# A retention layer and a gated MLP on one core: who loads, scales and turns each visit, and in which order

## The chip, the cores and the metric

The kernel runs on one core of one Trainium2 chip. The core has five engines with a queue of instructions each: TensorE (PE, matrix products and transposes), VectorE (DVE), ScalarE (ACT), GpSimd (POOL) and SyncE (SP, which here only issues transfers). Each queue runs in its order; an instruction that waits holds up everything behind it. ACT and POOL can issue transfers as well. The metric is the device time of one execution in microseconds, lower is better. Every time below is of this kernel before the change, either its timed runs or one profiled execution.

## The reference

For 8 batches, 8 heads, 576 positions and head size 64, the first half is a retention layer, scores masked by a decay and multiplied with the values, with no softmax. The second half is a gated MLP over the sequence; all inputs and the output are float32.

```python
scores = (1.0 / np.sqrt(D)) * np.matmul(q, k.transpose(0, 1, 3, 2))
gamma = 1.0 - 2.0 ** (-5.0 - np.arange(H))
Dmat = np.where(rel >= 0, gamma[:, None, None] ** rel, 0.0)      # rel = i - j
x = merge_heads(np.matmul(scores * Dmat, v))                      # 8 x 576 x 512
h = gelu_tanh(x @ w_in)                                           # 8 x 576 x 1024
u, v = h[..., :512], h[..., 512:]
v_n = (v - mean(v)) / np.sqrt(var(v) + 1e-6) * g_ln
v_s = np.einsum('ts,bsd->btd', w_sg, v_n) + b_sg[None, :, None]
out = x + (u * v_s) @ w_out
```

## The kernel before

**Visits.** The sequence of each pair of batches is cut into nine visits ("units"): eight of 256 positions by four heads of one batch, and one, number 4 of the nine (`MID`), of 64 positions of both batches with all heads. Four pairs give 36 units, 0 to 35. A unit loads its q, k and v (three transfers of 256 KB; the middle ones are six of 128 KB) into one of six float32 buffers. `scaled` (L504) then makes bf16 copies: q times its decay (`qs`, L534) and v times its decay (`vb`, L537) are products of 128x512, k is cast (`kb`, L530 on POOL, L528 on ACT for the first four units). PE must have q and k with the head size on the partitions. `turned` (L541) does it with eight PE transposes and one copy out of PSUM by DVE (L550) for units 0 to 19 (`TD = 20`); from unit 20 on SP issues one transposing DMA for each two units (L499).

**Retention.** `score` (L566) makes the products of q and k, DVE masks them (`ret`, L586), `states` (L596) adds k times v to the running states, and `outp` (L678) writes the unit's output from masked scores, values and states; ACT and DVE move it into the transposed activation `xT`. From unit 9 on (`i > JOIN`, with `JOIN = 8`) the score and the states of the next unit are issued in one step with the output of the present one; up to there they are steps of their own.

**MLP.** For each 128 rows `mlp_V` (L815) multiplies `xT` with the second half of `w_in` (four products of 512 columns), ACT applies gelu, DVE the statistics, POOL the root, ACT the normalization. `mlp_U` (L857) does the first half of `w_in`. `batch` (L878) multiplies with the 576x576 matrix `w_sg`, which is cast and turned once (`weights`, L447), gates, multiplies with `w_out` and adds x; `out` leaves in 256 KB pieces.

**The weights.** `w_in` is 2 MB of float32. `w_load` (L338) has POOL issue four transfers that turn it into bf16 on the way, two for each half, cut by rows. So a product with any column of a half needs both transfers of that half. `g_ln` and `b_sg` are loaded straight into columns, one float32 to each partition (L391, L396, L397), and prepared by `g_and_b`.

**The order.** Every step is a unit of `Plan` (L120) with an engine, a cost, what it reads and writes and what PSUM banks it takes. The table `TURN` gives each step a number; `Plan.emit` (L157) issues all steps in the order of these numbers, on whatever engine the step names, so the table fixes the order within each engine's queue. While it does so it keeps a running estimate, and where PE is estimated to be idle in the first 45 us it puts in products with a zero tile (`fill`, L300): they change no result and keep PE busy. Besides that the estimate only picks PSUM banks; the order is the table's. PE's order around the place that matters is, in units: turn 4, output 3, score 4, the first two `mlp_U` (of rows 0 to 255), turn 5, output 4, `mlp_V` 3, score 5, `mlp_V` 2, turn 6, and so on.

Of the kernel before, what the change touches and what calls it, by code (L numbers as in the profile page):

```python
# [19 lines left out]
    "b_col": [57],  # L20
    "b_rows": [0, 58],
    "b_tr": [72],
    "dtab": [33],
# [4 lines left out]
    "g_col": [76],  # L28
    "g_col1": [89],
    "g_inv": [90],  # L30
    "g_rows": [21, 109],
    "g_tr": [121],
    "gelu": [51],
# [6 lines left out]
    "ident": [4],  # L40
# [12 lines left out]
    "otu": [48, 55, 92, 110, 136, 162, 197, 268, 304, 335, 377, 419, 447, 472, 498, 539, 554, 582, 610, 640, 673,  # L53
        703, 718, 751, 782, 823, 839, 883, 914, 946, 969, 1004, 1026, 1053, 1068, 1101],
# [32 lines left out]
        807, 810, 945, 922, 940, 928, 1019, 1065, 1046, 1044, 1066, 1143, 1120, 1149, 1147],  # L87
    "wT": [244, 247, 273, 239, 276],
    "wT1": [326, 327, 293, 370, 287],
    "wT_b": [74],  # L90
    "wTp": [238, 237, 272, 233, 275],
    "w_in": [25, 38, 100, 82],
    "w_out": [320, 298, 333, 331],
# [923 lines left out]
```

## Time and profile before

| | us |
|---|---|
| median of 3 runs (lowest, highest) | 210.62 (210.22, 213.32) |
| the profiled execution | 209.62 |
| its span, first to last instruction | 207.9 |
| PE busy | 194.2 (93%) |
| DVE, ACT, POOL busy | 150.8, 134.7, 135.8 |
| DMA: 48.20 MB moved, mean | 232 GB/s |

The profiled execution took 1.0 us less than the median of the runs, and 1.7 us of it lie outside the span. The profile's windows give the busy time of each engine in a stretch, then the clock that PE was granted (1.00 is full), the mean busy share of the core's 16 DMA engines (over 1 where packets overlap), and GB/s. The chain is followed back from the last instruction, at each step to what released it. DMA_DIRECT2D rows on SPq or POOL are the issue of a transfer; its landing comes microseconds later.

### The profile page before, as it was taken

The page shows a single profiled execution, that of the slowest core. Times are in us where ns is not written, and L with a number is a line of the kernel's source. Part 1 is how long each engine was busy: PE and PEld are TensorE (multiplying, and loading weights), DVE is VectorE, ACT ScalarE, POOL GpSimd, SP SyncE. Part 2 cuts the span into 40 slices and gives each one's busy share as a digit, 9 for nine tenths or more (in the row PEclk, how much of TensorE's full clock was granted, in tenths as well). Part 3 has the DMA queues.
Part 4 walks back from the last instruction along what each step waited for, and adds up shares of the span by engine and source line. Part 5 has one row for each costly group of instructions (what it writes and reads, how often), then busy time and mean ns, then how long its engine had stood idle before and what let it go on. Part 6 is the DMA issues. An engine that isn't in the chain of part 4 may idle for free.

```text
span 207.9 us, 7429 instructions
## 1 busy us (share of the span) xinstructions
PE 194.2 (93%) x2994; PEld 124.2 (60%) x3027; DVE 150.8 (73%) x366; ACT 134.7 (65%) x316; POOL 135.8 (65%) x231
## 2 busy tenths in 40 slices
PE   6977949999999999999999999999999999999992
PEld 2543536768767776567745666575656565664651
DVE  1654953998987888978786658575869689896672
ACT  5363325799999846788589776765777377826400
POOL 6557989489769996759779865749846866123200
PEclk9999966999999999999999999999999999999999
DMA  5999999999999998695999899998998999895815
GB/s 145 267 203 192 228 274 302 300 296 309 192 277 251 290 330 213 175 241 136 265 210 299 229 175 199 271 317 208 255 267 236 201 175 262 192 189 195 249 54 202
DMA packets 98321, 48.20 MB, mean 232 GB/s; under 512 B 42288, under 2 KB 92720, under 8 KB 98288
## 3 DMA queue, kind: packets, MB, share of 16 engines
q1 hardware_dynamic: 97056, 46.56, 90.0%
q0 software_dynamic: 1088, 1.05, 3.6%
q8 instruction: 23, 0.38, 0.8%
q10 hardware_dynamic: 144, 0.13, 0.2%
q14 instruction: 10, 0.08, 0.1%
HBM read 32.79 MB, written 9.44 MB: 203 GB/s over the span
## 4 chain that ended last, share of the span: by engine, by line
PE 85%; DMA 8%; POOL 2%; issue 2%; DVE 1%; SPq 0%; DVEq 0%; POOLq 0%
PE p_d L890 19%; PE p_d L868 16%; PE p_d L923 14%; PE p_d L821 14%; PE p_oz L692 7%; PE p_d L547 4%; DMA w_in<-in_moe_w_in_dram 4%; PE p_s L572 3%; DMA vf<-in_v_dram 3%; PE p_d L926 2%; DMA qkf<-in_q_dram 1%; PE p_oz L605 1%; PE p_d L301 1%; PE p_d L460 1%; POOL vb L537 1%
## 5 line engine op out<-in xcount | busy, mean ns | idle before, releaser
L586 DVE TENSOR_TENSOR ret<-p_s,tri 128x512 bf16<-128x512 f32 x64 | 42.5, 681 | 3.2 <-PE p_s L572 3.0
L537 POOL TENSOR_TENSOR vb<-vf,gv 128x512 bf16<-128x512 f32 x36 | 37.6, 1046 | 6.9 <-DMA vf<-in_v_dram 6.0
L890 PE MATMUL p_d<-wT,vn 128*128 128x288 bf16 x256 | 40.5, 286 | 0.0
L868 PE MATMUL p_d<-xT,w_in 128*128 128x512 bf16 (+2 forms) x224 | 37.9, 314 | 2.1 <-DMA w_in<-in_moe_w_in_dram 2.1
L534 POOL TENSOR_TENSOR qkb<-qkf,gq 128x512 bf16<-128x512 f32 x35 | 36.5, 1047 | 4.3 <-DMA qkf<-in_q_dram 2.8
L821 PE MATMUL p_d<-w_in,xT 128*128 128x512 bf16 x126 | 34.8, 380 | 1.3 <-issue 0.5
L923 PE MATMUL p_d<-w_out,uT 128*128 128x512 bf16 (+1 forms) x137 | 34.5, 373 | 0.9 <-issue 0.5
L898 DVE TENSOR_TENSOR uT<-p_d,uT 128x288 bf16<-128x288 f32 x64 | 27.6, 448 | 6.1 <-PE p_d L890 4.8
L890 PEld LDWEIGHTS <-vn 128*128 128x128 bf16 x256 | 24.4, 98 | 7.1
L873 ACT ACTIVATE uT<-p_d 128x512 bf16<-128x512 f32 x36 | 21.2, 596 | 11.1 <-PE p_d L868 11.0
L853 ACT ACTIVATE vn<-vg,stat 128x512 bf16<-128x512 f32 x32 | 25.6, 814 | 3.8 <-POOL stat L840 3.7
L868 PEld LDWEIGHTS <-w_in 128*128 128x128 bf16 x224 | 19.4, 101 | 13.6 <-DMA w_in<-in_moe_w_in_dram 2.3
L838 POOL TENSOR_TENSOR stat<-stat,mhalf 128x1 f32<-128x1 f32 x36 | 20.2, 562 | 11.0 <-DVE stat L832 6.0
L824 ACT ACTIVATE vg<-p_d 128x512 f32<-128x512 f32 x36 | 20.9, 596 | 9.3 <-PE p_d L821 9.2
L829 DVE BATCH_NORM_STATS2 stat<-vg 128x6 f32<-128x512 f32 x36 | 24.6, 684 | 2.5 <-ACT vg L824 2.4
L530 POOL CAST qkb<-qkf 128x512 bf16<-128x512 f32 x32 | 19.5, 613 | 8.5 <-DMA qkf<-in_k_dram 5.8
L550 DVE COPY qkT<-p_d 128x1024 bf16<-128x1024 bf16 x20 | 13.7, 683 | 11.7 <-PE p_d L547 11.5
L923 PEld LDWEIGHTS <-uT 128*128 128x128 bf16 x148 | 13.7, 98 | 13.1
L821 PEld LDWEIGHTS <-xT 128*128 128x128 bf16 x144 | 13.0, 98 | 12.2 <-DVE xT L772 0.4
L837 POOL TENSOR_SCALAR stat<-stat 128x1 f32<-128x1 f32 x26 | 5.6, 217 | 20.7 <-DVE stat L830 15.6
L890 PE MATMUL p_d<-wT,vmid 128*128 128x288 bf16 x64 | 18.4, 287 | 0.0
L547 PE MATMUL p_d<-ident,qkb 128*128 128x128 bf16 x160 | 13.3, 229 | 1.0 <-POOL qkb L534 0.8
(103 smaller groups left out, 308.3 us busy)
## 6 DMA issues: line engine op xcount, KB each, us to landing
out_dram<-ob SPq DMA_DIRECT2D x35, 256.0 KB, 3.9
qkf<-in_q_dram SPq DMA_DIRECT2D x32, 256.0 KB, 5.4
qkf<-in_k_dram SPq DMA_DIRECT2D x32, 256.0 KB, 5.5
vf<-in_v_dram SPq DMA_DIRECT2D x32, 256.0 KB, 5.6
wsg<-in_moe_w_sg_dram SPq DMA_DIRECT2D x4, 288.0 KB, 5.1
w_in<-in_moe_w_in_dram POOLq DMA_DIRECT2D x4, 256.0 KB, 5.7
qkf<-in_k_dram SPq DMA_DIRECT2D x8, 128.0 KB, 5.1
qkf<-in_q_dram SPq DMA_DIRECT2D x8, 128.0 KB, 5.0
```

Source lines behind the costliest of these rows:

```text
L534: plan.add("POOL" if i else "DVE", 1010 if i else 700, key, lambda: eng.tensor_tensor(split(qs[a]), shape(qkf[l][:, 0, :]), gain(gq), op=A ...
L537: plan.add("POOL", 1010, key + 2, lambda: nc.gpsimd.tensor_tensor(shape(vb[a][:]), shape(vf[l][:]), gain(gv), op=Alu.mult), reads=rd(i, 2) ...
L547: nc.tensor.transpose(banks[0][:].bitcast(BF)[:, (x * KK + kk) * 128:(x * KK + kk + 1) * 128], src[:, kk * 128:(kk + 1) * 128], ident[:])
L586: nc.vector.tensor_tensor(ret[r][x][:].rearrange("p (s k j) -> p s k j", s=2, k=2), banks[0][:].rearrange("p (s k) j -> p s k j", s=2), tr ...
L821: nc.tensor.matmul(banks[0][:], xT[p % NX][:, m, kk, :], w_in[:, kk, F2:], start=(kk == 0), stop=(kk == KK - 1))
L829: nc.vector.bn_stats(st[:, 0:6], vg[g][:])
L853: nc.scalar.activation(vn[p % 2][m][:], vg[g][:], Act.Identity, scale=st[:, 8:9], bias=st[:, 9:10])
L868: nc.tensor.matmul(hu[:, c, :].rearrange("p (t j) -> p t j", j=128), w_in[:, kk, 128 * (x * per + c):128 * (x * per + c) + 128], xT[p % NX ...
L873: plan.add("ACT", 500, key, lambda banks, x=x: nc.scalar.activation(uT[p % NX][:, x * per:x * per + per, cols], banks[0][:].rearrange("p ( ...
L890: nc.tensor.matmul(banks[0][:, :HS], src[:, 128 * c:128 * c + 128], wT[e][j][:, half * HS:(half + 1) * HS], start=(j == 0), stop=(j == SB ...
L898: plan.add("DVE", 380, key, lambda banks, c=c, col=col: nc.vector.tensor_tensor(uT[x][:, c, col:col + HS], banks[0][:, :HS], uT[x][:, c, c ...
L923: nc.tensor.matmul(banks[0][:, :w], uT[x][:, c, r], w_out[:, c, x0:x0 + w], start=(c == 0), stop=late and c == KK - 1, skip_group_check=True)
```

## The change

- **Sides.** `Plan.add` may get several engines with a cost each, and a second table, `SIDE`, picks one for every single step. Of the 36 q products 7 now go to DVE (before 1), of the v products 8 (before 0); 13 of the k casts to ACT (before 4); 12 of the copies after the PE turn to ACT; the five copies that make the second `wT` from ACT to POOL; state copies in both directions. Six loads, and the last half output but one as before, are issued by ACT.
- **`w_in`.** Four float32 transfers of 512 KB, issued by SP and cut by columns, into the output buffers (three) and a new buffer `wst` (one); POOL casts the first three, ACT the last. A first `mlp_U` now needs one of the two pieces of its half. `mlp_V` of rows 0 to 255 is cut in two halves of 256 columns, one for each piece.
- **g and b** are loaded as nine rows of 128 and turned by one PE transpose with a float32 identity.
- **Turns.** `TD = 22`: units 20 and 21 go to PE too, seven transposing DMAs are left. `JOIN = 6`: units 7 and 8 are joined as well.
- **Buffers.** Unit i uses load buffer i mod 6 from the start; before, the first four shared two.
- **Order and estimate.** `TURN` is new throughout, the costs and the estimate of transfers are changed, and the fills are 61 instead of 37.

```diff
@@ class Plan
+        if isinstance(engine, dict):
+            sides, some = engine, emit
+            self.sides[len(self.units)] = sides
+            engine = self.side[name][mine] if name in self.side else next(iter(sides))
+            engine = {e[0]: e for e in sides}[engine[0]]
+            cost, emit = sides[engine], lambda *banks: some(engine, *banks)
...
-                self.idle(free[e], t)
+                self.idle(free[e], t + (350 if t < 32000 else 0))
...
-                    free[e] = max(t + cost, pipe - 1000)
-                pipe = max(pipe, t + cost + 600) + dma + (950 if issued == 2 else 0)
+                    free[e] = max(t + cost, pipe - 3000)
+                pipe = max(pipe, t + (900 if cost >= 1300 else cost + 600)) + 1.01 * dma + (600 if issued == 2 else 0)
@@ the tables
+    "qkT": "DDAAADADDAADDAAAADADDA",
+    "qs": "DDPPDPPDPPPPPPPDPPPPPDPPPPPPDPPPPPPP",
+    "vb": "PDPDDPPPPPPDDPPPPPPPPPPDPPDPPPPPPPDP",
+    "wT1": "PPPPP",
+    "w_in": "PPPA",
@@ the kernel
-    JOIN, TD = 8, 20
+    JOIN, TD = 6, 22
...
-        return (0, 1, 1, 0)[i] if i < 4 else (i - 2) % NL
+        return i % NL
...
-        plan.add("POOL", 770, (1 - half) * T0 + 10 + c, lambda: nc.gpsimd.dma_start(
-            w_in[:, c:c + 2, half * F2:(half + 1) * F2],
-            moe_w_in.rearrange("(c p) f -> p c f", p=128)[:, c:c + 2, half * F2:(half + 1) * F2]),
-            reads=[("ld", 1, 0, 0)] if half else [("vb", 1)], writes=[("w_in", half, c), ("w_in", half, c + 1)], dma=1500)
+        x = 2 * (1 - half) + c
+        part_ = wst[:] if x == 3 else obs[x][:].rearrange("p a f -> p (a f)").rearrange("p (k f) -> p k f", k=KK)
+        held = [] if x == 3 else [("ob", 2 * x), ("ob", 2 * x + 1)]
+        f0 = half * F2 + c * (F2 // 2)
+        plan.add("SP", 560, (1 - half) * T0 + 10 + c, lambda: nc.sync.dma_start(
+            part_, moe_w_in.rearrange("(k p) f -> p k f", p=128)[:, :, f0:f0 + F2 // 2]),
+            writes=[("wf", x)] + held, dma=1750)
+        plan.add({"ACT": 965, "POOL": 985}, None, (1 - half) * T0 + 10 + c, lambda e: copy(
+            e, w_in[:, :, f0:f0 + F2 // 2], part_),
+            reads=[("wf", x)] + held, writes=[("w_in", half, c)])
...
-        plan.add("SP", 600, -1.1 * T0, lambda: nc.sync.dma_start(
-            g_col[:], moe_g_ln.rearrange("(c p) -> p c", p=128)), reads=[("ld", 0, lb(2), 0)], writes=["g_col"], dma=300)
+        plan.add("SP", 500, -1.1 * T0, lambda: nc.sync.dma_start(
+            gb[:KK, :], moe_g_ln.rearrange("(c p) -> c p", p=128)), reads=["dtab"], writes=[("gb", 0)], dma=100)
...
-        eng = nc.gpsimd if i else nc.vector
-        plan.add("POOL" if i else "DVE", 1010 if i else 700, key, lambda: eng.tensor_tensor(
+        plan.add({"POOL": 1000, "DVE": 620}, None, key, lambda e: by[e].tensor_tensor(
             split(qs[a]), shape(qkf[l][:, 0, :]), gain(gq), op=Alu.mult),
             reads=rd(i, 0) + ["gq"], writes=[("qs", a)])
-        plan.add("POOL", 1010, key + 2, lambda: nc.gpsimd.tensor_tensor(
+        plan.add({"POOL": 1000, "DVE": 620}, None, key + 2, lambda e: by[e].tensor_tensor(
             shape(vb[a][:]), shape(vf[l][:]), gain(gv), op=Alu.mult),
             reads=rd(i, 2) + ["gv"], writes=[("vb", a)])
@@ the order: two lines of TURN
-    "w_in": [25, 38, 100, 82],
+    "w_in": [86, 89, 181, 179],
+    "wf": [45, 57, 153, 167],
```

What the tables do to the order is seen in three places. The first is SP's queue before, from the first transfers of unit 4 on; `qkf_63` and `vf_69` are unit 4, the next two buffers units 5 and 6, `qkf_66` unit 7. The transfers of `w_in` are not in it, since POOL issues them.

```order
17 L319 DMA qkf_63<-in_q_dram 64x8x64
18 L319 DMA qkf_63<-in_k_dram 64x8x64
19 L319 DMA qkf_63<-in_q_dram 64x8x64
20 L319 DMA vf_69<-in_v_dram 64x8x64 x2
21 L327 DMA qkf_64<-in_q_dram 128x4x128
22 L327 DMA qkf_64<-in_k_dram 128x4x128
23 L327 DMA vf_70<-in_v_dram 128x4x128
24 L327 DMA qkf_65<-in_q_dram 128x4x128
25 L327 DMA qkf_65<-in_k_dram 128x4x128
26 L327 DMA vf_71<-in_v_dram 128x4x128
27 L327 DMA qkf_66<-in_q_dram 128x4x128
28 L327 DMA qkf_66<-in_k_dram 128x4x128
```

SP's queue in the changed kernel at the same place: `qkf_66` is now unit 5, `qkf_61` unit 6, `qkf_62` unit 7, and `ob_146` and `wst` receive the first half of `w_in`.

```order
19 L367 DMA qkf_66<-in_q_dram 128x4x128
20 L367 DMA qkf_66<-in_k_dram 128x4x128
21 L367 DMA vf_72<-in_v_dram 128x4x128
22 L367 DMA qkf_61<-in_k_dram 128x4x128
23 L367 DMA qkf_61<-in_q_dram 128x4x128
24 L367 DMA vf_67<-in_v_dram 128x4x128
25 L383 DMA ob_146<-in_moe_w_in_dram 128x4x256
26 L383 DMA wst<-in_moe_w_in_dram 128x4x256
27 L367 DMA qkf_62<-in_q_dram 128x4x128
28 L367 DMA qkf_62<-in_k_dram 128x4x128
```

The half of `w_in` that `mlp_U` needs comes behind all of units 0 to 6 and ahead of unit 7. The second place is POOL's queue before, with the issues of its third and fourth transfer of `w_in` and the scaling of units 2 and 3 (`vb_77`, `vb_78`) around them.

```order
27 L537 TENSOR_TENSOR vb_77<-vf_68,gv 128x512
28 L339 DMA w_in<-in_moe_w_in_dram 128x2x512
29 L537 TENSOR_TENSOR vb_78<-vf_67,gv 128x512
30 L672 CAST zsA_95<-s_1_94 128x128
31 L401 TENSOR_SCALAR g_tmp<-g_col 128x4
32 L402 TENSOR_SCALAR g_inv<-g_col 128x4
33 L403 TENSOR_TENSOR g_tmp<-g_tmp,g_inv 128x4
34 L404 TENSOR_TENSOR g_col<-g_col,g_tmp 128x4
35 L339 DMA w_in<-in_moe_w_in_dram 128x2x512
```

POOL's queue in the changed kernel around the cast of the third piece; `vb_77` is the v product of unit 6 here, `vb_78` that of unit 7.

```order
42 L574 TENSOR_TENSOR qkb_74<-qkf_61,gq 128x2x4x64
43 L878 TENSOR_TENSOR stat_119<-stat_119,mhalf 128x1
44 L577 TENSOR_TENSOR vb_77<-vf_67,gv 128x512
45 L343 CAST zsB_98<-s_0_91 128x128
46 L343 CAST w_in<-ob_146 128x4x256
47 L878 TENSOR_TENSOR stat_120<-stat_120,mhalf 128x1
48 L878 TENSOR_TENSOR stat_118<-stat_118,mhalf 128x1
49 L343 CAST qkb_74<-qkf_62 128x2x4x64
50 L577 TENSOR_TENSOR vb_78<-vf_68,gv 128x512
```

The cast stands behind unit 6's q and v and ahead of unit 7's k. The third place is PE where the first `mlp_U` products stand. Before, they come right behind the transposes of `g_rows` and ahead of the turn of unit 5:

```order
668 L423 MATMUL p_d_173<-ident,g_rows 128x128
669 L868 LDWEIGHTS w_in
670 L868 MATMUL p_d_171<-xT_99,w_in 128x256
...
700 L868 MATMUL p_d_172<-xT_99,w_in 128x256
701 L547 LDWEIGHTS qkb_73
702 L547 MATMUL p_d_170<-ident,qkb_73 128x128
```

In the changed kernel they come behind the output of unit 5 (`vb_76`) and ahead of the turn of unit 7:

```order
1010 L725 LDWEIGHTS vb_76
1011 L725 MATMUL p_oz<-ret_1_84,vb_76 64x128
1012 L908 LDWEIGHTS w_in
1013 L908 MATMUL p_d_172<-xT_99,w_in 128x256
...
1077 L332 MATMUL p_d_173<-zero 128x512
1078 L587 LDWEIGHTS qkb_74
```

Between the two places PE has taken up the turns of units 5 and 6, outputs 4 and 5, scores and states of 5 and 6, and `mlp_V` of 2, 3 and 4. PE's order behind it is, in units: first, third and fifth `mlp_U`, turn 7, fourth `mlp_U`, output 6 with score 7, second `mlp_U`, turn 8, `mlp_V` 6 and 5, the last two `mlp_U` of this round, the turns of `w_sg`, output 7 with score 8, turn 9.

More of the change, by code (lines that the diff above doesn't have):

```diff
@@ L127, with __init__ @@
     HOP = {"PE": 205, "DVE": 135, "ACT": 150, "POOL": 110, "SP": 0}
-    FIRST = {"PE": 1300, "DVE": 900, "ACT": 2100, "POOL": 500, "SP": 350}
-    def __init__(self, pools, turn, fill):
+    FIRST = {"PE": 1300, "DVE": 900, "ACT": 800, "POOL": 500, "SP": 350}
+    def __init__(self, pools, turn, side, fill):
         self.units = []
+        self.sides = {}
+        self.side = side
         self.fill = fill
@@ L303, with copy @@
     xr_turn = [0]
-    plan = Plan({"s": p_s, "oz": [p_oz], "d": p_d}, TURN, fill)
+    plan = Plan({"s": p_s, "oz": [p_oz], "d": p_d}, TURN, SIDE, fill)
+    by = {"POOL": nc.gpsimd, "DVE": nc.vector}
+    queue = {"SP": nc.sync, "ACT": nc.scalar}
+    def copy(e, dst, src):
+        if e == "ACT":
+            nc.scalar.activation(dst, src, Act.Copy)
+        else:
+            by[e].tensor_copy(dst, src)
     T0 = 5300.0
@@ new lines, in g_and_b @@
+        plan.add("SP", 1000, -1.1 * T0 + 1, b_load, reads=["dtab"], writes=[("gb", 1)], dma=100)
+        plan.add("DVE", 80, 2 * T0, lambda: nc.vector.tensor_copy(identf[:], ident[:KK + SB, :KK + SB]), reads=["ident"], writes=["identf"])
+        u = plan.add("PE", 230, 2 * T0, lambda banks: nc.tensor.transpose(banks[0][:, :KK + SB], gb[:], identf[:]),
+                     reads=[("gb", 0), ("gb", 1), "identf"], writes=["gb_tr"], take=[("d", 1)])
+        plan.add("DVE", 100, 2 * T0, lambda banks: nc.vector.tensor_copy(gbc[:], banks[0][:, :KK + SB]), reads=["gb_tr"],
+                 writes=["g_col", "b_col"], give=[(u, [0])])
@@ L708, in outp @@
         reads = [("qkT", r), ("ret", r, 0), ("ret", r, 1), ("vb", a)] + inter_reads(i)
-        writes, take, cost = [("otu", i), "ozS"], [("oz", 1)], 350 if mid else 460 if n > 1 else 410
+        writes, take, cost = [("otu", i), "ozS"], [("oz", 1)], 390 if mid else 520 if n > 1 else 470
         if joined:
@@ L832, in bn @@
                 nc.vector.tensor_scalar(st[:, 8:9], st[:, 7:8], 1e-6, None, op0=Alu.add)
[L833 removed]
+        plan.add("DVE", 825 if pooled else 1010, key + 1, bn, reads=[("vg", g)], writes=[("st", g)])
         def root():
@@ L973 @@
         if not i:
-            for c in (0, 2):
+            for c in range(2):
                 w_load(1, c)
@@ L980 @@
         if i == 1:
-            for c in (0, 2):
+            for c in range(2):
                 w_load(0, c)
```

229 lines of the change are left out of this document (114 added, 115 removed), and 112 rows, old and new, of the table TURN.

## The prediction

> **What bounds the kernel now.** I read the page's busy times, then the windows, then the chain from the first `mlp_U` on, then the landings.
>
> ```profile
> span 207.9 us, 7429 instructions
> PE 194.2 (93%) x2994; PEld 124.2 (60%) x3027; DVE 150.8 (73%) x366; ACT 134.7 (65%) x316; POOL 135.8 (65%) x231
> L301 PE MATMUL p_d<-zero 128*128 128x512 bf16 x33 | 11.4, 461 | 1.7 <-DVE zero L962 1.2 <-issue 0.3
> ```
>
> ```profile
> 0.00:25.00 25.00, 20.14 (x278) 10.18 (x282) 13.05 (x34) 11.45 (x40) 17.00 (x38) 1.00 0.96 207
> 25.00:29.30 4.30, 1.62 (x53) 1.09 (x52) 3.64 (x11) 1.39 (x4) 3.96 (x8) 0.80 1.10 249
> 29.30:35.00 5.70, 5.62 (x51) 3.94 (x52) 0.81 (x2) 1.90 (x5) 5.02 (x7) 0.55 1.10 314
> 35.00:50.00 15.00, 14.90 (x296) 10.93 (x297) 13.57 (x36) 13.20 (x28) 11.25 (x17) 1.00 1.08 299
> 50.00:100.00 50.00, 48.99 (x869) 34.96 (x876) 42.34 (x105) 41.08 (x91) 40.11 (x61) 1.00 0.96 236
> 100.00:150.00 50.00, 49.52 (x790) 31.11 (x797) 34.75 (x86) 35.92 (x87) 36.76 (x62) 1.00 1.00 242
> 150.00:195.00 45.00, 44.52 (x608) 26.20 (x614) 35.60 (x81) 29.34 (x65) 21.72 (x43) 1.00 0.92 216
> 203.20:207.90 4.70, 0.73 (x7) 0.40 (x5) 1.25 (x3) 0.00 (x0) 0.00 (x0) 1.00 0.56 200
> ```
>
> From 35 us to the end PE does nothing but work: its idle time between 50 and 195 adds up to 1.97 us (1.01 + 0.48 + 0.48). Before that it waits and runs 11.4 us of fills, while the DMA engines are busy throughout (0.96, then 1.10). So the kernel is bound by transfers at first and by PE afterwards, and a change can gain in two ways only: less PE work, or PE at full work sooner. The place is the first `mlp_U`:
>
> ```profile
> 21.84 7.45 DMA w_in<-in_moe_w_in_dram
> ...
> 29.33 3.60 PE p_d L868 x16
> ...
> 35.79 0.97 PE p_d L821 x4
> 36.76 0.45 PE p_d L547 x8
> ...
> 38.10 0.46 PE p_oz L692 x24
> 38.56 0.22 PE p_s L572 x16
> 38.78 0.12 PE p_d L605 x16
> ...
> 49.40 0.98 PE p_d L868 x8
> ```
>
> ```profile
> PE p_d L868 <- DMA w_in<-in_moe_w_in_dram: 2.1, 1, 2.1
> ```
>
> The last transfer of `w_in` ends PE's wait at 29.33. The clock is then at 0.55 for 5.70 us, which costs 5.70 x 0.45 = 2.57 us. The last `mlp_U` of this round ends at 49.40 + 0.98 = 50.38. That is 21.05 us after the first, 18.48 at full clock.
>
> **The change part by part: the order around `mlp_U`.** PE now reaches the first `mlp_U` with turns 5 and 6, outputs 4 and 5, scores and states 5 and 6 and `mlp_V` 2, 3, 4 behind it. By the chain's pieces these are 2 x 0.45 + 2 x 0.46 + 2 x (0.22 + 0.12) + 3 x 0.97 = 5.41 us, now done while transfers are awaited. Of the 18.48 remain 13.07 from the first `mlp_U` to the same point.
>
> When can it begin? Its piece of `w_in` now comes behind all of units 0 to 6. The anchor is unit 7's k before, ahead of which units 0 to 6, all of `w_in` and unit 7's q had landed:
>
> ```profile
> L327 SPq DMA_DIRECT2D qkf<-in_k_dram x1: 841/841/841, 28.8 to 28.8; - x1
> ...
> DMA to landing us min/median/max: 5.2/5.2/5.2
> ```
>
> ```profile
> 2.00:10.00 8.00, 7.52 (x65) 3.50 (x64) 3.15 (x6) 3.65 (x22) 4.90 (x10) 1.00 1.01 262
> 10.00:22.00 12.00, 9.05 (x169) 4.97 (x170) 6.34 (x18) 5.82 (x15) 7.94 (x16) 1.00 1.04 192
> 29.30:45.00 15.70, 15.51 (x254) 11.19 (x258) 10.09 (x27) 10.29 (x22) 11.27 (x16) 0.84 1.07 292
> ```
>
> It landed at 28.8 + 5.2 = 34.0. Take away unit 7's q and k (2 x 0.262 MB at 292 GB/s, 1.8 us) and the fourth piece lands at 32.2; take away that piece (0.524 MB, 1.8 us) and the third lands at 30.4. The bytes are the same as before, and the DMA engines were already full, so I let nothing else move it. For bounds: units 0 to 6 and three pieces are 5.51 + 1.57 = 7.08 MB. From 2 us on, that is 29.0 at 262 GB/s and 38.9 at 192. I take 30.4, the value with a landing behind it. Then comes the cast, of 1024 columns:
>
> ```profile
> L530 POOL CAST qkb<-qkf 128x512 bf16<-128x512 f32 x32 | 19.5, 613 | 8.5 <-DMA qkf<-in_k_dram 5.8
> L528 ACT ACTIVATE qkb<-qkf 128x512 bf16<-128x512 f32 x4 | 2.5, 630 | 7.3 <-DMA qkf<-in_k_dram 7.3
> L534 POOL TENSOR_TENSOR qkb<-qkf,gq 128x512 bf16<-128x512 f32 x35 | 36.5, 1047 | 4.3 <-DMA qkf<-in_q_dram 2.8
> ```
>
> POOL 2 x 0.61 = 1.2, so `mlp_U` starts at about 31.7. The third product needs ACT's cast: 32.2 + 1.3 = 33.5, and the two before it last until 31.7 + 2 x 0.98 = 33.7, so it is just covered. That cast makes ACT wait at its head for `wst`, with unit 5's output behind it; nothing on PE needs this before `mlp_V` 5. On SP unit 7's loads and `w_sg` are queued behind the two pieces; the anchor prices that, since the same bytes were ahead of them before. Unit 7's k and v land near 34.0 and 34.9; with 0.6 and 1.0 on POOL, turn 7 waits some tenths, and output 6 is met in time. So the round ends at 31.7 + 13.1 + 0.4 = 45.2, against 50.38: **5.2 us earlier**.
>
> **The clock.** In the row from 25.00 the clock is already cut while PE works 1.62 of 4.30 us, and the longest wait on the list is 2.1 us. The Trainium skill ("TensorE: Matmul & The Clock Gate", section "Why this matters for your kernels") says that a drop needs an idle gap above some 3 us. By that, shorter gaps would leave the changed kernel at full clock; by this row sparse work is enough, and up to 2.6 us could return. I take no loss: 24 more fills stand in just this stretch. The fills cost nothing as long as transfers are later than they are.
>
> **Two more units turned by PE.** 2 x 0.45 = 0.9 us, near 100 us, where PE is full: all on the path. Their copies and the transposing DMA that goes cost PE nothing, since it waits for none of them there.
>
> **What I cost at nothing.** The halves of `mlp_V` 0 and 1 (eight short products more), g and b as rows with one transpose, the joined units 7 and 8 (the same products in fewer steps), free load buffers from the start: all lie before 31.7, beside transfers, or keep PE's work the same. If that cover is gone, they are tenths each. POOL's four issues of `w_in` go, and three casts of 1.2 come.
>
> ```profile
> L339 POOL DMA_DIRECT2D w_in<-in_moe_w_in_dram x4 | 3.3, 824 | 0.0
> L534 DVE TENSOR_TENSOR qkb<-qkf,gq 128x512 bf16<-128x512 f32 x1 | 0.7, 719 | 0.4 <-DMA qkf<-in_q_dram 0.4
> ```
>
> Fourteen products more on DVE take 14 x 0.72 = 10.1 us there and free 14 x 1.05 = 14.7 on POOL; DVE gives 12 copies to ACT. Engines that are not the bound; what could go wrong is a rival.
>
> **Sum.** -5.2 + 0.9 = -4.3 us: the profiled execution goes from 209.62 to 205.3. It lay 1.0 under the median of the runs, so **206.3 us**.
>
> **The rivals.** *The gain is bigger.* If the third piece lands at 29.0, PE has unit 6 by then too, and the round starts 1.4 us sooner; with nothing waited for behind it, 2 us: 204.3. At 299 GB/s throughout the piece would land at 25.7, 4.7 us before the forecast, which gives 201.6 as the utmost. For it: 4-byte loads and casting transfers are gone from the stretch at 192 GB/s. Against: the busy share there was 1.04, so slots were not empty.
>
> *The gain is given back after 50 us.* PE is 5 us ahead, transfers are not.
>
> ```profile
> 51.05 1.05 POOL L534 TENSOR_TENSOR qkb<-qkf,gq 128x512 bf16<-128x512 f32 x1
> ...
> 55.86 0.61 PE L547 MATMUL p_d<-ident,qkb 128*128 128x128 bf16 x8
> ```
>
> ```profile
> 45.00:60.00 15.00, 14.79 (x270) 11.41 (x271) 13.34 (x33) 14.67 (x28) 12.00 (x17) 1.00 1.05 271
> 60.00:80.00 20.00, 19.63 (x354) 13.95 (x356) 16.55 (x45) 15.77 (x41) 19.01 (x25) 1.00 1.15 286
> ```
>
> Unit 10's q was ready at 52.1 and turned at 55.86: 3.8 us of slack, less than 5.2. ACT was busy 14.67 of 15.00, POOL 19.01 of 20.00, DMA above 1. If all comes back: 206.3 + 4.3 = 210.6. Against: POOL gives 14 products and 9 casts away.
>
> *DVE holds POOL up.* A DVE product with both inputs in SBUF beside POOL's work is seen once:
>
> ```profile
> 7.62 0.72 DVE L534 TENSOR_TENSOR qkb<-qkf,gq 128x512 bf16<-128x512 f32 x1 [0.41 <-DMA qkf<-in_q_dram]
> 7.73 0.96 POOL L339 DMA_DIRECT2D w_in<-in_moe_w_in_dram  x1
> ...
> 10.40 0.76 POOL L339 DMA_DIRECT2D w_in<-in_moe_w_in_dram  x1
> ```
>
> The issue beside it took 0.96 instead of 0.76. If each such product stopped POOL for its 0.72, the six more that come up to unit 7 (q of 1, 4, 7, v of 1, 3, 4) would delay POOL, and with it the cast of `w_in`, by 4.3 us: 210.6 again. The Trainium skill ("SBUF — State Buffer", section "Who interferes with whom") states this rule: such a DVE instruction and a GpSimd one that reads SBUF exclude each other for the whole instruction. The 0.2 us seen speaks for a part of it, no more.
>
> *Slower: `w_in` comes too late.* It is behind units 4 to 6 now. If the stream runs as between 10 and 22 us, the third piece lands at 38.9, `mlp_U` starts 8.5 us later than forecast, and PE, dry from 31 on, loses the clock as well: 206.3 + 8.5 = 214.8, up to 217.4. It decides from a landing at 34.7 on, where the 4.3 us are eaten.
>
> **How the numbers follow.** A measurement tells about 2% (4.2 us) from no change; faster is below 206.4. The forecast, 204.5 to 208.5, has 0.45, split by that bound about in half (0.22 faster, 0.23 same). The bigger gain has 0.22, given back 0.13 (same), DVE on POOL 0.08 (0.06 same, 0.02 slower), late `w_in` 0.12 (0.11 slower, 0.01 same). Faster 0.44, same 0.43, slower 0.13. For the range I leave out the slower end and the best of the bigger gains: 202.5 to 211.5.
>
> **What would show it.** Right: the first `mlp_U` (L908) between 31 and 33, clock 1.00 from 10 us on, the last of its round at 45 to 46, and no PE wait above 0.5 us behind it. Wrong: PE waits on `w_in` past 34.7; a clock below 1 between 20 and 45; PE idle above 1 us in any 10 us after 50, with turns late; or POOL products beside DVE's clearly longer than 1.05.

## The result: no gain, and about 1% slower

Side by side on one chip the changed kernel took 210.07 us (median of 20 runs, 209.08 to 211.03), the kernel before 209.26 (20 runs, 207.09 to 213.91). The ratio is **1.0114, 95% interval 1.0089 to 1.0139**: no gain, and slower by more than the measurement is uncertain, though by less than 2%. (The ratio leaves out runs of the kernel before that lay over 1.5% above its fastest.) The profiled execution took 209.76 us against 209.62, with the same span. The forecast was 206.3, and 4.3 us less in the profile.

The page's busy times and its row of fills, of the kernel after:

```profile
span 207.9 us, 7572 instructions
PE 197.4 (95%) x3042; PEld 126.8 (61%) x3076; DVE 155.9 (75%) x373; ACT 140.3 (67%) x318; POOL 128.3 (62%) x226
L332 PE MATMUL p_d<-zero 128*128 128x512 bf16 x57 | 18.3, 425 | 2.4 <-DVE zero L1001 1.2
```

The windows of the kernel after, cut as before (length, busy time of PE, PE's weight loads, DVE, ACT, POOL, then clock, DMA share, GB/s):

```profile
0.00:25.00 25.00, 22.07 (x325) 12.16 (x330) 16.57 (x42) 14.43 (x46) 14.77 (x37) 1.00 1.00 243
25.00:29.30 4.30, 4.09 (x69) 2.33 (x70) 2.44 (x7) 2.37 (x5) 3.35 (x5) 1.00 1.09 328
29.30:35.00 5.70, 5.65 (x120) 3.60 (x119) 5.06 (x17) 4.43 (x9) 3.69 (x6) 1.00 1.14 311
50.00:100.00 50.00, 48.81 (x907) 34.03 (x914) 40.01 (x95) 41.50 (x92) 40.60 (x56) 1.00 1.06 271
100.00:150.00 50.00, 48.20 (x730) 30.40 (x738) 37.60 (x92) 35.96 (x84) 32.88 (x65) 1.00 0.94 198
```

The clock no longer falls (it was 0.80 and 0.55 in the second and third row), and transfers run faster before 30 us. But PE is busier by 3.2 us over the span (197.4 against 194.2), with 6.9 us more of fills (18.3 against 11.4; the trace holds 57 of the 61), and between 100 and 150 us it shows 1.3 us less than the kernel before did there.

The first `mlp_U` (L908) is in the chain of waits of the kernel after:

```profile
26.39 1.40 PE p_d L332 x6
27.79 0.45 PE p_d L587 x8
28.23 0.32 PE p_oz L725 x24
...
33.61 0.34 PE p_oz L725 x24
33.94 2.75 PE p_d L908 x32
```

It starts at 33.9, not 31.7, and PE did not wait for `w_in` there: from 25 us on it was at work, six fills of it in one piece of 1.40 us on the chain itself. The turn of unit 9 starts at 47.15, where the kernel before has it at 50.83. That is a lead of 3.7 us, of which 0.6 mean nothing, since a batch step that stood ahead of this turn stands behind it now. At the end nothing is left of it.

Where it went is seen when the same outputs are laid side by side. The table gives the start of an output on PE in the traces. The second row is an experiment below: the kernel before with ten more fills, in an execution at full clock. The row "ahead" says how much more PE work the changed order has placed in front of that output (turn 0.60 us, `mlp_V` 0.86, `mlp_U` 0.89, batch step 0.63, output product 0.98, worked out from the busy times, so good to some tenths); "same work" is the start less the second row's, less "ahead".

```
output                      9       12       22       23       35    span
before, as profiled       58.75    73.43   117.65   123.72   182.99  207.9
before, ten more fills    56.02    70.70   114.92   120.99   180.26  205.2
after                     54.40    71.28   117.73   123.75   183.19  207.9
ahead in after            -0.99    +0.79    +3.09    +1.38    +1.36
after, same work          -0.63    -0.21    -0.27    +1.39    +1.57
```

The two upper rows differ by 2.73 us at every output of the table: what the profiled execution of the kernel before lost, it lost before 35 us, and 2.57 of it by the clock, by the prediction's rows. Against the same kernel at full clock the changed one leads by only 0.63 at output 9, and has lost that and 1.57 more by output 35, 2.2 in all. There it also has 1.36 us more work behind it, most of it the two turns: 1.57 + 1.36 = 2.93, of which 2.7 are left in the spans.

### The profile page after: what moved, and what is told of

The parts are those of the page before. It is cut to its first block, busy times and chain, and to the rows that moved or that the text cites. A ratio compares the mean times of both kernels' runs of the same rounds, so it can differ in the third digit from the quotient of the medians.

```text
span 207.9 us, 7572 instructions
## 1 busy us (share of the span) xinstructions
PE 197.4 (95%) x3042; PEld 126.8 (61%) x3076; DVE 155.9 (75%) x373; ACT 140.3 (67%) x318; POOL 128.3 (62%) x226
## 3 DMA queue, kind: packets, MB, share of 16 engines
q10 hardware_dynamic: 3312, 1.57, 2.8%
## 4 chain that ended last, share of the span: by engine, by line
PE 86%; DVE 7%; ACT 2%; issue 2%; DVEq 0%; ACTq 0%
PE p_d L930 17%; PE p_d L908 14%; PE p_d L857 14%; PE p_d L963 14%; PE p_oz L725 7%; PE p_d L332 7%; PE p_d L587 5%; PE p_s L612 4%; PE p_d L966 2%; PE p_oz L645 1%; DVE qkb L574 1%; PE p_d L512 1%; DVE ret L626 1%; DVE uT L938 1%; DVE qkT L343 1%
## 5 line engine op out<-in xcount | busy, mean ns | idle before, releaser
L857 PE MATMUL p_d<-w_in,xT 128*128 128x512 bf16 (+1 forms) x134 | 34.4, 366 | 1.7 <-issue 1.0
L908 PE MATMUL p_d<-xT,w_in 128*128 128x512 bf16 (+2 forms) x224 | 35.6, 303 | 0.0
L574 POOL TENSOR_TENSOR qkb<-qkf,gq 128x512 bf16<-128x512 f32 x29 | 30.6, 1058 | 0.6 <-DMA qkf<-in_q_dram 0.4
L577 POOL TENSOR_TENSOR vb<-vf,gv 128x512 bf16<-128x512 f32 x28 | 29.5, 1057 | 2.1 <-DMA vf<-in_v_dram 2.0
L864 ACT ACTIVATE vg<-p_d 128x512 f32<-128x512 f32 x36 | 21.4, 601 | 9.9 <-PE p_d L857 8.1
L908 PEld LDWEIGHTS <-w_in 128*128 128x128 bf16 x224 | 18.9, 98 | 10.6
L857 PEld LDWEIGHTS <-xT 128*128 128x128 bf16 x152 | 14.0, 98 | 12.6 <-issue 0.7
L332 PE MATMUL p_d<-zero 128*128 128x512 bf16 x57 | 18.3, 425 | 2.4 <-DVE zero L1001 1.2
L343 POOL CAST qkb<-qkf 128x512 bf16<-128x512 f32 x23 | 14.6, 637 | 4.6 <-DMA qkf<-in_k_dram 3.4
L785 ACT ACTIVATE xs<-p_oz 128x256 f32<-128x256 f32 x24 | 9.2, 383 | 9.7 <-PE p_oz L725 4.1
```

The lines of the kernel that those rows point to most:

```text
L332: nc.tensor.matmul(bank[:], zero[:, :128], zero[:], start=True, stop=True, skip_group_check=True)
L574: plan.add({"POOL": 1000, "DVE": 620}, None, key, lambda e: by[e].tensor_tensor(split(qs[a]), shape(qkf[l][:, 0, :]), gain(gq), op=Alu.mul ...
L577: plan.add({"POOL": 1000, "DVE": 620}, None, key + 2, lambda e: by[e].tensor_tensor(shape(vb[a][:]), shape(vf[l][:]), gain(gv), op=Alu.mul ...
L857: nc.tensor.matmul(banks[0][:, y * w:y * w + w], xT[p % NX][:, m, kk, :], w_in[:, kk, F2 + y * w:F2 + y * w + w], start=(kk == 0), stop=(k ...
L864: plan.add("ACT", 500, key, lambda banks: nc.scalar.activation(vg[g][:], banks[0][:], Act.Gelu_apprx_tanh), reads=[("hv", i), ("hw", i)], ...
L908: nc.tensor.matmul(hu[:, c, :].rearrange("p (t j) -> p t j", j=128), w_in[:, kk, 128 * (x * per + c):128 * (x * per + c) + 128], xT[p % NX ...
```

## The experiments

Each ratio is to the kernel before, run beside it.

**Fills on the path, or fills that hold the clock?** The changed kernel without its last 20 fills:

```diff
-FILL_END = 45000
+FILL_END = 22000
```

> The changed kernel without the 20 fills that stand in PE's queue from the turn of unit 4 on (between 23.4 and 36.9 us of its trace). Theory 1, fills on the path: in that stretch PE was never idle for more than 0.2 us, so each fill in front of a step that was ready delayed the first mlp_U; it should start at 32.0 to 33.0 instead of 33.88, the time should fall by 1 to 2 us, to 208.0 to 209.0 (ratio to the kernel before 0.994 to 0.999). Theory 2, the fills hold the clock: without them the granted clock falls below 1 somewhere between 24 and 36 us, as in the kernel before (0.80, then 0.55), and what is gained is lost again: 210 to 212.

209.26 us, ratio 1.0107 (1.0063 to 1.0150). Its windows and chain:

```profile
25.00:29.30 4.30, 3.90 (x102) 2.44 (x101) 3.90 (x11) 3.60 (x10) 4.16 (x7) 1.00 1.00 295
29.30:35.00 5.70, 4.65 (x89) 3.38 (x90) 5.33 (x17) 4.51 (x10) 4.22 (x7) 1.00 1.13 314
```

```profile
31.79 0.47 issue
32.26 0.32 PE p_oz L725 x9
32.59 2.75 PE p_d L908 x32
...
53.53 0.09 PE p_oz L645 x10
53.63 1.04 issue
54.67 0.25 PE p_oz L645 x6
```

The clock stays at 1.00 without these fills, so in this order they hold nothing: theory 2 falls. The first `mlp_U` comes 1.35 us earlier, and at output 9 the lead in the same work grows from 0.63 to 2.19. So far theory 1. But output 35 starts only 0.69 us earlier (182.50 against 183.19), and the 208.0 to 209.0 that it expected were missed. 1.04 us go at 53.63, in the middle of a group of 16 products, by a stop for which the profile shows no release. While PE neared it, this answer for 51.5 to 54 us shows a transfer on the queue of instructions:

```profile
q8 instruction: 1, 0.02, 2.9%
```

This fetch (16 KB) ran from 52.0 to 53.2. Two more runs ask whether the stop belongs to the step or to a row of code, which here is one instruction of PE, a product or a weight load. One keeps five of the 20 fills, the other leaves out three early ones too:

```diff
-FILL_END = 45000
+FILL_END = 23500
```

> The changed kernel without its last 15 fills only (5 of the 20 taken away in the first run stay: ten more rows of code on PE ahead of everything after 25 us). In the run without late fills PE stopped for 1.04 us at 53.6 us in the middle of a group of 16 products of unit 11's states, after the tenth, and in the run with the product moved at the same one, for 1.21; the products wait for nothing, and a transfer of 16 KB on the queue of instructions ran from 52.0 to 53.2. Theory, PE waits for its own code: the place is a row number, so with ten rows more the stop comes five products earlier, after the fifth of the same group, and is shorter by what the five fills delay PE. Rival, the stop belongs to that step (a bank, a semaphore the profile does not show): it stays after the tenth.

```diff
-FILL_END = 45000
+FILL_END = 22000
-        lo = max(lo, s[0], 1500)
+        lo = max(lo, s[0], 2790)
```

> The changed kernel without the 20 late fills and without three of the ten fills ahead of the first turn (six rows of code fewer). Theory, PE waits for its own code: the stop near 53.6 us comes three products later, after the thirteenth of the same group of 16. Rival: it stays after the tenth. Time: 208.5 to 209.7, as without late fills; if the first turns now start earlier, up to 0.5 less.

With five fills back: 208.67 us, ratio **1.0057** (1.0011 to 1.0104). No stop is seen, neither after the fifth product nor after the tenth; PE comes to this group at 54.02, 0.66 later than in the first run (53.36). With three early fills less: 209.33 us, 1.0075 (1.0034 to 1.0116), and in its chain:

```profile
54.30 0.12 PE p_oz L645 x13
54.42 0.15 issue
54.57 0.22 PE p_oz L645 x3
```

The break is after the thirteenth product, as the row of code demands, not after the tenth. The traces of these runs say more than that. In the first run and in the one with three early fills less, the first row behind the stop is the 1729th that the trace records on PE, weight loads included. In the first run the break of 0.47 at 31.79, just ahead of the first `mlp_U`, is of the same kind: the row behind it is the 961st, and 1729 - 961 is 768, three times 256; the 24 fetches of 16 KB in that trace, for 6120 recorded rows, make 255 rows to a fetch. Each of these three rows starts 1.45 to 1.55 us after its fetch has ended (1.45, 1.53, 1.55). With five fills back PE comes to the 1729th row 1.66 us after its fetch has ended, and does not stop. So PE had run up to the end of the code that it had, and being earlier there bought nothing.

Fifteen late fills cost about 1.2 us: 1.0114 to 1.0057 by the ratios, whose intervals overlap, and 1.57 to 0.36 by the same work at output 35.

**What the clock is worth in the kernel before.** The changed kernel's rule for fills there, and then only ten of them, in the sparse stretch:

```diff
-                self.idle(free[e], t)
+                self.idle(free[e], t + (350 if t < 32000 else 0))
```

> The kernel before with the changed kernel's rule for fills (350 ns more of them ahead of each PE step planned before 32 us; 62 in place of 37), nothing else. Theory 1: in the kernel before, the first mlp_U waits for w_in until 29.3, so fills ahead of it are free; they keep the clock at 1.00 from 25 to 35 us, where it lost 2.6 us, and the time falls by 1.5 to 2.5 us, ratio 0.988 to 0.993. Then the clock is a part of the gain that has nothing to do with the new order. Rival: the clock of the kernel before falls in some executions only, and the median gains under 0.5 us (ratio 0.998 or more); or fills delay work there too and the ratio is above 1.

```diff
-                self.idle(free[e], t)
+                self.idle(free[e], t + (350 if 19000 < t < 32000 else 0))
```

> The kernel before with ten more fills only, those that the changed kernel's rule would add between 19 and 26 us of the plan (ahead of the turns of units 3 and 4, outputs 2 and 3, scores 3 and 4 and the first mlp_U). Theory: 62 fills held the clock in all executions but cost work time early; ten in the sparse stretch hold it at less cost: mean granted clock 0.995 or more in all executions, and the median falls to 206.2 to 206.8, where the executions of the kernel before with the clock at 0.997 or above lie (205.9 to 206.9). Rival: the clock falls in some executions all the same, or the fills cost as much as they hold: 207 or more, ratio 0.998 or more.

207.02 us, ratio 1.0008 (0.9969 to 1.0046), and 207.84 us, 1.0017 (0.9968 to 1.0065), where the kernel before had medians of 207.21 and 208.79. Ten fills suffice in the profiled execution:

```profile
25.00:29.30 4.30, 3.52 (x67) 1.85 (x65) 3.83 (x13) 1.43 (x4) 3.42 (x8) 1.00 1.09 261
29.30:35.00 5.70, 5.70 (x108) 4.24 (x106) 3.41 (x9) 4.29 (x10) 5.70 (x9) 1.00 1.06 308
50.00:100.00 50.00, 50.00 (x918) 34.92 (x913) 41.36 (x104) 39.35 (x91) 39.49 (x60) 1.00 1.06 251
```

No ratio below 1 comes of it. In both runs the theory was missed and the rival came true, since the ratio compares with the kernel before's faster executions, and these lose little or nothing by the clock. In 73 executions of it beside these runs (one more, at 492 us, left out), 51 show a mean clock under 0.996 and have a median of 209.15 us, 22 show 0.996 or more and have 206.6. The difference, 2.55 us, agrees with the loss that the prediction read from the trace (2.57). Ten fills gain 0.95 us by the medians on their chip, the 25 more gain 0.19 on theirs. What is gained is that fewer executions lose clock, not a faster execution: no version beat the kernel before beyond the uncertainty. With ten fills 10 of 12 executions kept the clock at 0.996 or more, with 25 more 11 of 12. The changed kernel kept it in all 26 of its executions, with a median of 209.8: at equal clock it is 3.2 us slower than the kernel before (3.1 on the one chip where both have such executions on record, 209.66 against 206.60).

**Two more units turned by PE.** Undone in the changed kernel, and done alone in the kernel before (in both, the table of places follows):

```diff
-    JOIN, TD = 6, 22
+    JOIN, TD = 6, 20
```

> The changed kernel with units 20 and 21 turned by the transposing DMA again, as in the kernel before (20 units by PE). Theory 1: the two turns are work on a full PE, 2 x 0.60 us by the time that 16 more of these transposes add after 47 us: 210.07 - 1.2 = 208.9 (ratio about 1.005). Rival: the transposing DMA of this pair lands late in this order and PE waits for it by more than 0.5 us: 209.6 or more.

```diff
-    JOIN, TD = 8, 20
+    JOIN, TD = 8, 22
```

> The kernel before with units 20 and 21 turned by PE (22 in place of 20), as the change does, and nothing else. Theory 1: PE is full there, so it costs the two turns, 0.9 to 1.2 us: ratio 1.004 to 1.006. Rival A: PE waits there for something anyway and the turns are free, ratio 0.998 to 1.002. Rival B: DVE's two more copies and the lost head start of the transposing DMA delay PE further: ratio above 1.008.

Alone: 208.96 us, ratio 1.0030 (0.9980 to 1.0080), undecided by the time, but clear in the trace: against the run with ten fills, its outputs 5 to 17 start 2.19 us later each (its execution lost clock before 35 us, and has 1.00 from there on), outputs 18 to 34 start 3.26 to 3.28 later. The two turns cost 1.07 us, as theory 1 had it. Undone: 212.18 us, 1.0257 (1.0211 to 1.0303), slower than the changed kernel by 2.2 in the spans (210.1 against 207.9). Theory 1 was missed; the rival had the time, but not the cause, since PE waits for no transposing DMA there. The trace has 0.9 us gained on the changed kernel between outputs 16 and 18, and waits that eat it: 1.3 for POOL's state at output 21, and 1.2 early, for a product of DVE. DVE's and POOL's rows around it, the kernel with 20 turns:

```profile
22.75 2.30 DVE L573 TENSOR_TENSOR qkb<-qkf,gq 128x512 bf16<-128x512 f32 x1
```

```profile
21.66 1.28 POOL L484 COPY vmid<-vmid 64x512 bf16<-64x512 bf16 x2
22.91 1.04 POOL L573 TENSOR_TENSOR qkb<-qkf,gq 128x512 bf16<-128x512 f32 x1
23.90 0.60 POOL L342 CAST qkb<-qkf 128x512 bf16<-128x512 f32 x1
24.45 0.75 POOL L342 CAST zsA<-s 128x128 bf16<-128x128 f32 x1
```

The product takes 0.68 alone. Here it is on record from 22.75 to 25.05, beside four instructions of POOL that follow each other with a gap of 0.03 us at most, as if POOL had let go only at about 24.5. In the changed kernel the same product took 0.80; there POOL's next work waited 0.36 for q and left it a gap. The opposite of the change, 18 turns on the kernel before with ten fills, was expected to beat both:

```diff
-    JOIN, TD = 8, 20
+    JOIN, TD = 8, 18
```

> The kernel before with the ten fills that held its clock, and with units 18 and 19 turned by the transposing DMA too (18 by PE in place of 20), the opposite of the change. Theory 1, each turn by PE is 0.5 us on a full PE: 1.07 us (what the two more turns cost in the kernel before) faster than with the ten fills alone, 206.0 to 206.8 median, faster than both kernels. Rival: the DMA's pair comes too late for its scores in this stretch, where the DMA engines' share is 0.9 to 1.1, and PE waits 1 us or more.

211.90 us, ratio 1.0179 (1.0118 to 1.0241). The rival was right; the list of waits has:

```profile
PE p_s L571 <- DMA qkT<-qkb: 4.9, 1, 4.9
```

This DMA was issued only at 89.96, and PE went on at 96.88.

**DVE's products.** The eight late ones back on POOL in the changed kernel; the same eight given to DVE in the kernel before:

```diff
-    "qs": "DDPPDPPDPPPPPPPDPPPPPDPPPPPPDPPPPPPP",
+    "qs": "DDPPDPPDPPPPPPPPPPPPPPPPPPPPPPPPPPPP",
-    "vb": "PDPDDPPPPPPDDPPPPPPPPPPDPPDPPPPPPPDP",
+    "vb": "PDPDDPPPPPPPPPPPPPPPPPPPPPPPPPPPPPPP",
```

> The changed kernel with its eight DVE products after unit 7 (q of units 15, 21, 28, v of 11, 12, 23, 26, 34) on POOL again, as in the kernel before; DVE keeps the seven early ones. Theory 1: on DVE such a product stands in front of the steps that PE waits for (1.36 us at 71.2, where it and a POOL product hold each other up, and 0.60 at 119.9, each on the chain of waits). Without them PE's idle time from 50 to 195 us falls from 3.4 to about 2.4, the time by 0.5 to 1.0, to 209.1 to 209.6. Rival: POOL, with 8.4 us more, gets late itself: idle 3.4 or more, 210.1 or more.

```diff
-        eng = nc.gpsimd if i else nc.vector
...
+        dve = i in (0, 15, 21, 28)
+        eng = nc.vector if dve else nc.gpsimd
...
+        dve_v = i in (11, 12, 23, 26, 34)
+        eng_v = nc.vector if dve_v else nc.gpsimd
```

> The kernel before with the eight products after unit 7 that the change gives to DVE (q of units 15, 21, 28, v of 11, 12, 23, 26, 34) on DVE, at their old places in the order. Theory 1, DVE products stand in front of steps that PE waits for, and DVE and POOL hold each other up: PE's waits from 45 to 195 us, none above 0.3 in that kernel now, grow to 0.5 to 2 us, ratio 1.003 to 1.010. Rival: POOL's relief is worth as much as DVE's load costs: ratio 0.997 to 1.002.

In the kernel before: 210.07 us, ratio **1.0117** (1.0034 to 1.0200), with the clock at 1.00 in the profiled execution: theory 1 in the mechanism, and above its range. The two longest waits of PE behind 45 us, and the first of them in the chain:

```profile
PE p_d L824 <- DVE uT L901: 1.0, 1, 1.0
PE p_d L824 <- DVE qkT L553: 0.9, 1, 0.9
```

```profile
118.65 2.60 issue
121.25 0.05 DVEq L535
121.30 0.04 issue
121.34 0.69 DVE qkb L535
122.03 0.20 DVE xT L762
122.23 0.37 DVE uT L901
122.61 0.04 issue
122.65 1.02 PE p_d L824 x4
```

DVE does its work in the order written. The product L535 (q of unit 28) kept it for 2.6 us without work, and `uT`, for which PE waited, stood behind it. The profile does not name what it waited for. In the run with ten fills the same product stands on POOL and waits there too, 1.57 us until 119.96, put down to the transposing DMA that reads the buffer it writes; but that stopped only POOL, and PE has no wait there. In the changed kernel, the products back on POOL: 213.73 us, 1.0321 (1.0278 to 1.0363). Of the two waits at 120 to 124 us the one of 0.7 went, as theory 1 had it, and the one of 0.4 stays; but there is a new one, and behind it a loss of clock:

```profile
PE p_oz L645 <- POOL vb L577: 3.4, 1, 3.4
```

```profile
60.00:80.00 20.00, 16.64 (x257) 11.72 (x246) 10.03 (x27) 11.63 (x26) 15.02 (x19) 0.83 1.15 288
```

So the rival was right for the time. Its chain ahead of this wait:

```profile
61.52 6.63 DMA qkf<-in_k_dram
...
69.10 1.01 POOL vb L577
```

It was not for want of room: POOL is busy for 15.02 of these 20 us. It stood 3.06 us until 63.62 for DVE's statistics (3.03 in the changed kernel), had work behind work after that (1.62 of it one of the copies `wT1`, which the change had given it), and k's transfer, whose cast stands ahead of this product, landed only at 68.15. A smaller edit: no late fills, and only one product, v of unit 26, placed behind the mask that it stood in front of:

```diff
-        714, 683, 721, 754, 748, 839, 882, 844, 927, 982, 952, 1010, 1027, 1068],
+        714, 683, 721, 754, 763.5, 839, 882, 844, 927, 982, 952, 1010, 1027, 1068],
```

> The changed kernel without the 20 late fills (as the first run), and with DVE's product for v of unit 26 placed behind the mask of the scores that it stood in front of (at 119.8 us in the changed kernel's trace), nothing else. Theory 1, a DVE product in front of steps that PE waits for: the two waits of PE at 120 to 124 us (0.7 for ACT's copy of an output, 0.4 for DVE's normed output) fall to 0.5 or less together, and the time by 0.6 to 1.1 us against the run without this move: ratio to the kernel before 1.005 to 1.008 in place of 1.0107. Rival: the waits come from ACT's queue (its cast of k ahead of the copy), and stay above 0.9 together, ratio 1.009 or more.

209.99 us, ratio 1.0123 (1.0049 to 1.0196): no gain to be seen in the time, whose spread on that chip was wide. In the trace the wait of 0.7 for ACT's copy is gone and the 0.4 for the normed output stays; from output 22 to 23 it loses 1.05 us of same work where the run without the move loses 1.66. The gain of 0.6 is lost in the opening, where PE waits 0.9 for POOL's q and 0.7 for DVE's statistics, on rows that the edit leaves as they were. So the place is right by the trace, and the size of the move is too small to tell by the time.

**Room on POOL by giving `wT1` back to ACT.** Three runs, the first on top of the products on POOL, each other on top of the one before it, beside the changed kernel once more:

> The changed kernel once more, unedited, as the base for the three other runs on the same chip. Both theories: 209.1 to 211.0 as before, clock 0.996 or more in every execution, while the kernel before spreads again from 205.5 (clock 1.00) to 211 (clock 0.98).

209.66 us, 1.0116 (1.0065 to 1.0167), the first result again.

```diff
-    "wT1": "PPPPP",
+    "wT1": "AAAAA",
```

> The changed kernel with its eight late DVE products on POOL (as in the run with products on POOL) and, new, the five copies for the second set of spatial weights (wT1, 3.5 and 2.0 us of POOL at 51 to 67 us) on ACT again, as in the kernel before. Theory: it was these copies that left POOL no room for the products; with them on ACT the wait of 3.4 us for v near 70 us and the loss of clock behind it go, the waits at 120 to 124 us stay away: 208.0 to 209.2, 0.5 to 1.5 us faster than the changed kernel. Rival: ACT, busy some 7.5 of 8 us between 52 and 60, is late by the 5 x 1.16 us: PE waits for ACT by more than 1 us between 50 and 75, and the time is 210 or more.

```diff
-FILL_END = 45000
+FILL_END = 22000
```

> The run with products on POOL and copies on ACT, and also without the 20 late fills. Theory: the fills are worth what they were worth alone, 0.2 to 0.6 us, since the engines behind PE set the pace after 50 us: 207.6 to 208.9. Rival: with the products off DVE nothing holds PE up later, and all of the 1.4 us by which the first mlp_U came earlier without the fills reaches the end.

```diff
-    JOIN, TD = 6, 22
+    JOIN, TD = 6, 20
```

> The run with products on POOL, copies on ACT and no late fills, and also with units 20 and 21 turned by the transposing DMA again. Theory: without the other waits the two turns are worth their 0.9 to 1.2 us: 206.6 to 207.8, level with the kernel before at full clock. Rival: as when this was done alone, the order is made for 22 turns and PE waits for what the DMA delivers: 1 us or more above the run without it.

214.64, 212.21 and 212.44 us, ratios 1.0350 (1.0294 to 1.0407), 1.0223 (1.0177 to 1.0268) and 1.0245 (1.0192 to 1.0298): all three theories fell. PE's wait for POOL's v only shrank, from 3.4 to 1.9 in each of them, and ACT is full instead, as the first of them shows:

```profile
60.00:70.00 10.00, 9.01 (x142) 5.15 (x142) 6.49 (x18) 9.96 (x23) 4.20 (x7) 1.00 0.99 258
```

What the late fills cost is larger here (214.64 to 212.21), and no worth of the two turns is to be seen. So the copies were not what kept POOL late: without them it is busy for 4.20 of these 10 us, and still it stands behind DVE's statistics (2.76 and 3.04 us) with the products behind them in its queue. In none of the runs that moved work between DVE, POOL and ACT here did the time fall. That the assignments hold only together with an order made for them is what this suggests; no run made a new order to show it.

## Why the prediction was wrong

The profiled execution was forecast at 205.3 us and took 209.76. Of this, about 2.0 us were missing at output 9 already, 2.2 were lost between there and output 35, and 0.2 are the turns.

**Where it failed first: "The fills cost nothing as long as transfers are later than they are".** Transfers were not later. The fourth piece of `w_in` landed at 30.8, not 32.2, by this answer on its tile (issue at 24.1, 6.7 to landing):

```profile
L383 SPq DMA_DIRECT2D wst<-in_moe_w_in_dram x1: 685/685/685, 24.1 to 24.1; - x1
...
DMA to landing us min/median/max: 6.7/6.7/6.7
```

PE itself was late. The timeline of the kernel after, where unit 6's q and k are made and turned:

```profile
27.31 1.04 POOL L574 TENSOR_TENSOR qkb<-qkf,gq 128x512 bf16<-128x512 f32 x1
27.33 0.61 ACT L341 ACTIVATE qkb<-qkf 128x512 bf16<-128x512 f32 x1
...
30.14 1.25 PE L332 MATMUL p_d<-zero 128*128 128x512 bf16 x5
31.23 0.61 PE L587 MATMUL p_d<-ident,qkb 128*128 128x128 bf16 x8
```

The fills were written into its queue by the plan's times, and here five of them stand ahead of a turn that had been ready since 28.35. The first `mlp_U` came at 33.88 instead of 31.7, and of this 1.35 us are the fills, as their removal shows; the other 0.8 stays without them, and 0.47 of it is there the break at 31.79. POOL's cast of the third piece was late for the same reason: it stood at 31.91, and at 30.31 without the late fills. From there on the sum was right: from the first `mlp_U` to turn 9 it took 13.3 us, where 13.5 were forecast.

**"5.2 us earlier".** Of this, 2.57 was the clock, and that was right for the execution that it was read from (2.73 by the outputs). The order's part, 2.6, came out as 0.63 at output 9; without the late fills it is 2.19, so the mechanism was right, and most of its size was eaten by the fills.

**"+1.0 to the median".** The profile was taken as a stand-in for the runs. But the clock loss is not in every execution of the kernel before, and the ratio compares with those that have little of it. A gain that consists in the clock is worth only as much as the share of executions that lose it.

**"Engines that are not the bound; what could go wrong is a rival".** DVE's products were costed at nothing after 50 us. The eight late ones cost the kernel before 1.2% (0.3 to 2.0) when given to DVE alone, since such a product can stand waiting in front of work that PE needs. This is the second step that failed. The rival "given back after 50 us" had the right place (2.2 us of the same work between output 9 and output 35) and a chance of 0.13; that its 210.6 lies so near the measured 210.07 is in part luck, since it gave as the cause transfers and ACT's and POOL's time. In the changed kernel the part that is shown is 0.6 us, at 120 us, and for that it is DVE's queue; how the rest of the 2.2 divides between DVE's products, the other changed sides and the order is left open, since no run undid them without making another engine late.

**"DVE holds POOL up".** I read 0.2 us as a sign of a part of the lock only. Longer overlaps show more, and both ways: in the kernel after, a POOL product that began while DVE's ran took 1.49 instead of 1.04, and a DVE one beside two of POOL's 1.45 instead of 0.68:

```profile
71.14 1.45 DVE L574 TENSOR_TENSOR qkb<-qkf,gq 128x512 bf16<-128x512 f32 x1
...
119.78 0.68 DVE L577 TENSOR_TENSOR vb<-vf,gv 128x512 bf16<-128x512 f32 x1
119.87 1.49 POOL L574 TENSOR_TENSOR qkb<-qkf,gq 128x512 bf16<-128x512 f32 x1
```

The Trainium skill ("SBUF — State Buffer", section "Who interferes with whom") says that who comes first keeps the ports for the whole instruction and the other is blocked; these numbers agree, with 0.45 us lost by POOL and 0.77 by DVE. But the rival's price, POOL held for 0.72 by each such product and `w_in`'s cast 4.3 us late by it, did not come: the cast stood behind a wait for DVE's statistics, not behind a DVE product, and was done 0.9 us before PE came to need it.

**Two turns.** Forecast 0.9, measured 1.07: right, and all on the path. **The clock.** 1.00 where it had fallen, as forecast, but by PE's own work, not by the late fills. "`w_in` comes too late" had nothing in it. Of what was to show it right, only the clock came. Of what was to show it wrong, two came: POOL products beside DVE's clearly above 1.05, and PE idle above 1 us in ten (0.7 and 0.4 at 122 to 124).

## What to carry to other kernels

Before a gain is summed against one profile, ask which part of that profile's time other executions do not have; here more than half of the forecast (2.57 of 4.3 us) was a clock loss that 3 in 10 executions escape. Work that is put into an in-order queue to fill a wait must be shown to lie in the wait, at the times of the trace and not of the plan. An engine with spare time is not free for an operation that can wait for data: what counts is who stands behind it in its queue.

## What the hardware showed unexpectedly

PE can be stopped by its own code: for 0.47, 1.04, 1.21 and 0.15 us in three runs, at rows 961 and 1729 of those recorded on it, each row starting 1.45 to 1.55 us after a 16 KB fetch had ended, and three products later in the work when six rows of code were taken out ahead of it. The clock fell in the kernel before with no wait of PE above 2.1 us, and in the run with two more turns (to 0.71 from 30 to 35 us) with none above 1.25; with ten fills (3.52 us of 4.30 busy, waits of 0.4 at most) it stayed. The Trainium skill ("TensorE: Matmul & The Clock Gate", section "Why this matters for your kernels") warns of idle gaps above 3 us; in this kernel sparse work was enough, and 51 of 73 executions lost clock. And a DVE product of two SBUF inputs, 0.68 us alone, took 2.30 beside a POOL that had work behind work.
